# Identity products in free PSUM tiles, W^T copies behind both transposes, and a new written-out order in an RWKV-7 + cosine-gated MLP kernel

## The chip, the cores and the metric

One Trainium2 chip, one core. The time is the device time of one execution in microseconds (us). TensorE (PE; its weight loads are shown as PEld) multiplies into PSUM, VectorE (DVE) and ScalarE (ACT) read PSUM and write SBUF, GpSimd (POOL) works on SBUF, and SyncE (SP) and ACT issue the transfers between HBM and SBUF. Each engine takes its instructions in the order in which the program gives them; between engines they wait on semaphores.

## The reference

An attention block of the RWKV-7 kind with 4 batches, 8 heads, 768 steps and head dimension 40 runs first. Its output, as 3072 tokens of 320 values, goes through a two-layer MLP with h * cos(h) between the layers.

```
for t in range(S):
    y[t] = r[t] @ state
    Sa = state @ a[t]
    state = state * w[t] - outer(Sa, b[t]) + outer(v[t], k[t])
x = y as (3072, 320)
h = x @ w_in            # 320 -> 2048
out = (h * cos(h)) @ w_out   # 2048 -> 320
```

The MLP's weights come as 64-bit floats; everything is computed in 32-bit floats.

## The kernel before, in words

**Units.** The 768 steps are cut into chunks of 64 and the batches into pairs, which gives 24 units u; a unit is 64 steps of two batches, 128 partitions. Units 2n and 2n+1 make up group n, 256 tokens of the MLP. Within a chunk the recurrence is written as matrix products and one triangular inverse for each head.

**Segments of a unit.** `pw` (`p1_w`) transposes the decay w of two units; `pa` (`p1_a`) transposes a and multiplies it by w; `rw` (`over_w`) takes 1/w on DVE; `pb` and `pn` (`p1_b`, `p1_n`) transpose b over w and form the products of a and b, which fill the triangular systems; `inv` and the items `i` solve these on DVE for four units at a time, in 31 steps (the first four units in blocks of half the size, with the products `below` in `F` and `S` between); `H` and `R` add the lower blocks (tiles `beside`). Then come `v` and `k` (transposes of v, r and k), `g` (`gram`), `ag`, `xa`, `s`, `z` (the state of the next chunk and the output `yt`), `t` and `q` (the state transposed, times r). `T` and `X` bring `yt` to the MLP's layout `xT` by way of HBM, `Y` does it for the first two units on TensorE. `K` is work on POOL ahead of `k`.

**The decay.** For the first four units w is the plain input, and its running product is made by a scan on DVE behind the transpose; `p1_w` keeps both units of the pair in one tile `wT` of PSUM. For each unit of the pair in turn it transposes (four products against `ident`), copies or scans to `wb` in SBUF, and makes `wc` on POOL. From unit 4 on the running product along time is made beforehand in another layout (`scan`, `wj`, `sd`, `ws`: two sweeps on DVE and POOL, stored to HBM and loaded again), and `p1_w` copies the transposed tile to `wb` on ACT (line 371).

**Weights.** The 64-bit weights are rounded to 32 bits in 20 blocks of 512 columns. `f` fetches a block's words; the items `c` take the steps of `rounded` in the order of the list `w_names`: `taken` (sign on ACT, line 264; mantissa and exponent on DVE, lines 265 and 266; the exponent's power on ACT, line 269), `mantissa` (DVE, line 272), `product` (DVE, line 278; POOL, line 281). In the program's order `taken` of block n+2 stands behind `mantissa` of block n+1.

**The MLP.** Pieces `M` run in a fixed sequence: `first_a` and `first_b` (tiles `ph`, 256 tokens by 512 of the 2048 columns), then `second` (tiles `po`) for the piece before. The items `r` are the cosine and the product on ACT and DVE between them (`turns`, `gT`); `o` stores the output. A piece asserts that its weights are ready.

**PSUM.** Three pools of two tiles each: `ps_a` with tiles of two banks (tag `at`), `ps_h` and `ps_o` with one bank. `at` and `one` take a tile; the first writer waits until the last reader of the buffer's tile before is done.

**What sets the order.** The string `PLAN` is an order written out item by item; the loop at the end runs through it and emits each item's instructions, so an engine's order is that of the items. `L` items load a unit's inputs (`Lk3`: k of unit 3), by SP, or by ACT where the name ends in `a`. A transfer waits in its queue until its buffer is free, and what stands behind it in the queue waits too.

**TensorE's clock.** The profile lists a granted clock; it is 1.00 in most of the run and 0.50 in stretches of the first part.

Of the kernel before, what the change touches and what calls it, by code (L numbers as in the profile page):

```python
# [20 lines left out]
def kernel(  # L21
# [64 lines left out]
    G = {"rest": [], "outs": []}  # L86
# [150 lines left out]
    def rounded(m, dst, src):  # L237
# [23 lines left out]
        def taken():  # L261
            hi, mant = t["words"][:, :, 1], dst.bitcast(I32)
            t["sign"] = sb2.tile([P, DM], F32, tag="ot", name="sign").bitcast(BF16)[:, :WID]
            nc.scalar.activation(t["sign"], hi, ACTF.Sign)
            nc.vector.tensor_scalar(mant, hi, 0xFFFFF, None, ALU.bitwise_and)
            nc.vector.tensor_scalar(
                hi, hi, 20, 0x7FF, ALU.logical_shift_right, ALU.bitwise_and
            )
            nc.scalar.activation(hi, hi, ACTF.Relu, bias=to_bits, scale=2.0**23)
# [13 lines left out]
        return fetch, taken, mantissa, product  # L283

    def weights():
# [5 lines left out]
        def put(dst, src):  # L291
            if wide:
                work.append(rounded(len(work), dst, src))
                return

            def fetch():
                for rows, cols, part in src:
                    nc.sync.dma_start(dst[rows, cols], part)

            none = lambda: None  # L300
            work.append((fetch, none, none, none))
# [36 lines left out]

    def at(name):
        return ps_a.tile([P, 2, 512], F32, tag="at", name=name)  # L340

    def one(pool, name):
        if pool is None:
            return at(name)[:, 0]
        return pool.tile([P, 512], F32, tag="h" if pool is ps_h else "o", name=name)
# [12 lines left out]
    def p1_w(u):  # L358
        ps = at("wT")
        for i in range(2):  # L360
            turned(ps[:, i], nat["w", u + i])
            if u < 4:
                nc.scalar.copy(G["w1"][:, i, :, 0:1], b4(ps[:, i])[:, :, 0:1])
                nc.vector.memset(ps[:, i, ::C], 0.0)
            wb = ring.tile([P, 4 * P + 1], F32, tag="wb", name="wb")
            if u < 4:
                nc.vector.tensor_tensor_scan(
                    wb[:, 1:], ps[:, i], flat(G["w1"][:, i]), 0.0, ALU.mult, ALU.add
                )
            else:  # L370
                nc.scalar.copy(wb[:, 1:], ps[:, i])  # L371
# [476 lines left out]
    def first_a(g, j):  # L848
        assert not G["rest"]
        G["ph"] = [ps_h.tile([P, 512], F32, tag="h", name="ph").rearrange("p (f t) -> p f t", f=2)  # L850
                   for _ in range(2)]
# [53 lines left out]
    def second(g, j, i):  # L905

        if j == 0:
            G["po", i] = ps_o.tile([P, 512], F32, tag="o", name="po")
# [178 lines left out]
    with tc.manual_schedule():  # L1087

        w_work = weights()
        w_names = ["t0", "t1", "m0"]  # L1090
        follower = {4: 7, 5: 8, 6: 9, 11: 14, 12: 15, 13: 16, 14: 17, 15: 18, 17: 19}
        follower.update({m: m + 3 for m in range(7, 11)})
        for n in range(len(w_work)):
            w_names.append(f"p{n}")
            if n + 1 < len(w_work):
                w_names.append(f"m{n + 1}")
            if n + 2 < len(w_work):
                w_names.append(f"t{n + 2}")
        w_count = [0]

        def w_item():
# [6 lines left out]
            w_work[m]["tmp".index(name[0]) + 1]()  # L1108
# [27 lines left out]
        def inv_begin(q):  # L1136
# [8 lines left out]
            f1 pw0 Lk0 pa0 f3 pw2 pb0 pa2 pn0 lo0 pb2 inv0 pn2 i lo2 i i f0 i c Lv0 i i Lr0a K0 i f2 scan1 i  # L1145
            Lk1 i i c k0 v0 c i i i Lv1a i i g0 i wj1 i c K1 F0 ag0 c i F1 Lr1 c S1 S0 xa0 k1 H0 c f4 sd1 f5
            v1 c c R0 g1 F3 c s0 ag1 Lk2 c ws1 c c f6 Lv2 xa1 z0 K2 Lw4a s1 c S3 Lr2 Lb5a c c Y0 z1 c F2 c c
            k2 Y1 wf2 t2 c c c Lw5 v2 c S2 c Lb4 M c M La4 c r r La5 g2 r c r scan2 H1 c c r r c c Lv3 M pw4
            c rw5 ag2 q2 c rw4 M Lw7a c c xa2 R1 r M Lk3 c c r s2 c Lr3 c K3 r M pb4 r Lw6a z2 c r pa4 c wj2
            k3 c pn4 Lv4 r Lb6a c M Lb7 c rw7 v3 lo4 M Lk4 rw6 sd2 c g3 c T2 pw6 M La6a K4 r r t3 La7 c ag3  # L1150
            r q3 c c M pb6 xa3 c c c t4 c r r s3 Lr4 c c pa6 ws2 r z3 pn6 c c M c inv1 M c lo6 c r k4 X2 i r
            r i i T3 M v4 Lk5 r X3 i Lv5 i r i M r i i g4 M Lr5 i i M i r i Lr6 r wf3 ag4 i Lw9 q4 i r i r r
            M Lw8a i i M r t5 i M i Lb9a xa4 v5 M Lv6 i i r i i Lb8 r i i K5 M r i i r r i r i i i i k5 La8
            La9 q5 M Lk6 i pw8 M i g5 v6 M Lv7 H2 scan3 H3 r pa8 La11 rw8 R2 ag5 Lr7 r s4 M r Lb10 r rw9 z4
            Lw10 xa5 r wj3 M Lw11 r pb8 s5 K6 Lb11 M t6 pw10 rw10 sd3 pn8 La10 T4 pa10 lo8 ws3 M Lb12 rw11 r
            Lk7 r R3 z5 r inv2 pb10 X4 r La13 pn10 k6 M r r i La12 T5 X5 i g6 i M lo10 i i o K7 i i i ag6 q6
            Lw13 i i o Lb13a i i M v7 xa6 M r i r r i i s6 Lw12 r Lr8 t7 M i i M r i r k7 Lr9 z6 g7 Lk8 rw12
            M M i r r Lv8 wf4 i i ag7 q7 r i r M i xa7 i v8 K8 r o r M i k8 i i pw12 g8 T6 Lv9 rw13 t8 M M i
            i r Lv10 i i s7 i i Lk9 r pb12 i M ag8 r q8 r M r xa8 Lr10 H4 r pa12 z7 R4 M K9 Lw14 t9 v9 T7 X6
            Lk10 H5 s8 X7 M pn12 Lb15 scan4 Lw15 Lb14 r r z8 M Lv11 rw14 lo12 r M r r r k9 pw14 La14 g9 v10  # L1160
            M ag9 T8 wj4 q9 M o r La15 K10 Lk11 R5 Lb16 sd4 rw15 xa9 r M inv3 pa14 X8 k10 r M r r Lb17 g10
            s9 r M pb14 o Lr11 z9 pn14 M t10 r r r o i Lr12 i i M r M ag10 r i r Lv12 lo14 i T9 q10 M xa10 i
            M K11 i ws4 s10 v11 r M X9 i r M r La16 i r k11 Lw17 La17 r i r i i i i Lw16 z10 Lv13 g11 M M
            Lk12 r K12 pw16 i T10 Lr13 t11 r M i Lk13 i r M r ag11 i q11 r r i M i pa16 xa11 M r r rw16 r
            v12 i r i r v13 rw17 M M r Lr14 s11 i k12 La19 i i M M r z11 g12 r M wf5 r M i r r i r Lb18 pb16
            t12 i i i i i i M M X10 ag12 K13 q12 r i scan5 r Lk14 r M r Lw19 r r M H6 Lw18 xa12 inv4 M M T11
            R6 H7 r r r r r M s12 pn16 r M o k13 X11 lo16 M Lv14 t13 Lb19 La18 o v14 g13 z12 M r r ag13 K14
            T12 q13 r Lr15 r wj5 rw19 r M pw18 xa13 M k14 sd5 R7 pa18 r rw18 M t14 g14 s13 M r pb18 r Lv15 r
            z13 pn18 r M i r i ws5 Lk15 i i i K15 M i lo18 ag14 q14 r X12 i M v15 Lb20 i i xa14 i M i La21 r
            k15 s14 r i r M o Lv16 M r i i i T13 X13 r r i t15 Lk16 Lw21 i La20 g15 z14 Lr16 M i M r r ag15  # L1170
            q15 r i r i Lb21 Lr17 M M r o K16 r i v16 rw21 i Lw20 M k16 xa15 rw20 M r g16 i r r i s15 r Lk17
            Lb23 M i M T14 i r t16 r pw20 z15 i Lw22 pa20 M M r i ag16 q16 Lv17 r i M i r i i r r r Lr18 M
            Lv18 i t17 M i M xa16 r K17 v18 M pb20 r r H8 M Lk18 r r H9 R8 r T15 M M r s16 r r pn20 M lo20
            X14 M Lw23 Lr20 k17 X15 Lb22 o o inv5 v17 r r r z16 pw22 M T16 M r g17 R9 r r M K18 r ag17 r r
            Lk19 rw23 rw22 q17 M k18 M Lv19 La22 La23 M xa17 r X16 r r pa22 r r M M r o g18 s17 M pb22 z17
            pn22 M r r Lr19 i i lo22 r t18 r i i i K19 M M ag18 r r q18 i i M M xa18 r Lk20 i M i T17 r Lv20
            M r r r i X17 v19 v20 i r M t19 o s18 M r k19 i r z18 g19 r r M T18 r M r ag19 q19 M M i r xa19
            r i i r r M r Lv21 M r i i o K20 k20 i i M i i M g20 r Lr21 i s19 M i i r M r o r X18 r z19 r i
            t20 M Lv22 ag20 i i q20 M i r t21 Lk21 r r M M r Lr22 r T19 K21 i X19 i r i M xa20 M v22 r r v21
            M r i M i k21 i H10 r r Lk22 r M q21 Lr23 g21 M H11 r R10 r r M M ag21 r r s20 r M z20 xa21 M  # L1180
            s21 r T20 K22 r r X20 t22 r M M r k22 Lk23 z21 R11 r M Lv23 g22 M ag22 q22 r K23 r r o M o r T21
            r M X21 t23 r M xa22 M v23 r r r r k23 M r M s22 g23 r M ag23 q23 M xa23 r r r z22 s23 M r M r r
            M M r T22 z23 r r o o M X22 r M r r M M T23 r r r r M M r X23 r M M r r r r r r M M M M r r M r
            r r r M M o M r r M r r r o M r M M M r M r r r r r M o M o
# [16 lines left out]
        for n, (name, kind) in enumerate(zip(names, kinds)):  # L1201
            if kind == "M":
# [13 lines left out]
            else:  # L1216
# [6 lines left out]
                done.add(name)  # L1223
        assert not w_names and not inv_names and not G["rest"] and not G["outs"]
# [29 lines left out]
```

## Time and profile before

| what | value |
|---|---|
| median of 3 runs | 802.54 us (802.45 to 803.6) |
| the profiled execution | 800.9 us |
| its span, first to last instruction | 799.2 us |
| mean granted TensorE clock | 0.943 |
| PE busy | 730.2 us (91%), 11908 matmuls |
| DVE busy | 498.4 us (62%) |
| ACT busy | 416.4 us (52%) |
| POOL busy | 187.0 us (23%) |
| first piece of the MLP (`ph`) starts | 84.9 us |
| chain that ended last, by engine | PE 78%, DVE 11%, ACT 6%, issue 2%, DMA 2%, POOL 1% |

The page gives busy time by engine, the span in 40 slices (busy tenths and the granted clock), the chain of work that ended last, and groups of instructions. Lines of a timeline or chain start with the start in us and the length in us; "x32" is the number of instructions taken together. Most products are recorded at line 75 (`mm`) and transposes at line 350, so tiles' names tell the groups apart. A line of a wait reads: who waited, at which line, for whom, us in total, how many times, and the longest. In tables by stretches the numbers in brackets count instructions.

### The profile page before, as it was taken

To read this page: it belongs to the slowest core of one execution; us is meant where nothing else is said; L and a number is where in the kernel's file an instruction comes from. 1 tells how busy PE (TensorE), PEld (TensorE's weight loads), DVE (VectorE), ACT (ScalarE), POOL (GpSimd) and SP (SyncE) were. 2 spreads that over 40 slices of the span, in tenths; PEclk is the share of its full clock that TensorE was granted. 3 is DMA by queue.
4 is the path that set the end of the run, shared out by engine and by line. 5 is a ranking of instruction groups with operands and counts; after the bars stand their busy time and mean duration, and the time that the engine had idled before them with its cause. 6 is when DMAs were issued, how large, how long until landed. Compare 5 with 4: busy or idle time off the path is not lost.

```text
span 799.2 us, 27403 instructions
## 1 busy us (share of the span) xinstructions
PE 730.2 (91%) x11908; PEld 577.9 (72%) x11908; DVE 498.4 (62%) x965; ACT 416.4 (52%) x762; POOL 187.0 (23%) x320
## 2 busy tenths in 40 slices
PE   4568688899988999999999999999999999999995
PEld 4457566677776777877777777787878777777773
DVE  6686877698777864576864579733554863433221
ACT  1434656665474456563557464456464456454442
POOL 5244454320530233202232112221011012301000
PEclk8557898899899999999999999999999999999998
DMA  9444745553345204441322342321211210201000
GB/s 145 119 90 115 176 117 116 142 112 42 66 101 108 51 22 89 83 104 26 69 42 62 86 82 43 58 52 29 47 45 26 54 34 5 58 16 36 19 17 17
DMA packets 180912, 54.33 MB, mean 68 GB/s; under 512 B 156344, under 2 KB 176440, under 8 KB 180792
## 3 DMA queue, kind: packets, MB, share of 16 engines
q1 hardware_dynamic: 167000, 50.45, 28.8%
q10 hardware_dynamic: 13792, 2.13, 1.8%
q8 instruction: 94, 1.54, 0.8%
q14 instruction: 26, 0.21, 0.1%
HBM read 41.68 MB, written 10.81 MB: 66 GB/s over the span
## 4 chain that ended last, share of the span: by engine, by line
PE 78%; DVE 11%; ACT 6%; issue 2%; DMA 2%; POOL 1%; SPq 0%; ACTq 0%; DVEq 0%; POOLq 0%
PE ph L75 25%; PE po L75 24%; PE dps L75 4%; PE x0ps L75 4%; PE beside L75 3%; PE vT L350 2%; PE gram L75 2%; PE sps L75 2%; PE nps L75 2%; PE aps L350 1%; PE wT L350 1%; PE bT L350 1%; PE sT L690 1%; PE kT L350 1%; DVE inv L519 1%
## 5 line engine op out<-in xcount | busy, mean ns | idle before, releaser
L75 PE MATMUL po<-w_out_sb,gT 128*128 128x320 f32 x768 | 223.0, 441 | 0.0
L75 PE MATMUL ph<-xT,w_in_sb 128*128 128x256 f32 x768 | 185.4, 390 | 6.6 <-DVE gT L896 6.6
L75 PEld LDWEIGHTS po<-w_out_sb,gT 128*128 128x128 f32 x768 | 142.3, 191 | 57.4 <-issue 3.7
L75 PEld LDWEIGHTS ph<-xT,w_in_sb 128*128 128x128 f32 x768 | 142.8, 193 | 34.7 <-issue 14.1
L885 ACT ACTIVATE turns<-ph,rnd 128x512 f32<-128x512 f32 x96 | 62.6, 686 | 132.6 <-PE ph L75 130.2
L889 DVE SCALAR_TENSOR_TENSOR turns<-turns,ph 128x512 f32<-128x512 f32 x96 | 63.9, 681 | 84.5 <-ACT turns L885 84.4
L896 DVE TENSOR_TENSOR gT<-ph,turns 128x512 f32<-128x512 f32 x96 | 65.0, 686 | 45.9 <-ACT turns L893 45.8
L787 POOL TENSOR_TENSOR qz<-qz,wc 128x160 f32<-128x160 f32 x44 | 21.1, 482 | 227.9 <-DVE qz L786 226.2
L893 ACT ACTIVATE turns<-turns,half_pi 128x512 f32<-128x512 f32 x96 | 69.4, 723 | 3.1
L892 ACT ACTIVATE turns<-turns 128x512 f32<-128x512 f32 x96 | 60.4, 629 | 17.6 <-DVE turns L889 17.0
L519 DVE TENSOR_TENSOR inv<-inv,inv_tmp 128x31 f32<-128x31 f32 (+15 forms) x155 | 58.3, 376 | 5.3
L515 DVE TENSOR_TENSOR inv_tmp<-u,inv 128x31 f32<-128x31 f32 (+15 forms) x155 | 54.6, 352 | 3.1
L75 PE MATMUL ph<-xT,w_in_tail 64*64 64x256 f32 (+1 forms) x704 | 52.1, 384 | 0.0
L384 DVE RECIPROCAL rw<-nat_w 128x320 f32<-128x320 f32 x20 | 42.6, 2139 | 0.0
L802 POOL TENSOR_TENSOR yt<-yt,wb 128x512 f32<-128x512 f32 x24 | 31.7, 1321 | 42.0 <-DVE yt L797 42.0
L385 POOL TENSOR_TENSOR bn<-nat_b,rw 128x320 f32<-128x320 f32 x22 | 19.4, 882 | 92.1 <-DVE rw L384 54.1
L738 DVE COPY x<-x0ps 128x416 f32<-128x416 f32 x24 | 14.1, 587 | 39.2 <-ACT x L737 39.0
L760 DVE TENSOR_TENSOR sm<-sps,su 128x256 f32<-128x256 f32 x48 | 18.1, 419 | 30.9 <-ACT sm L755 28.8
L75 PEld LDWEIGHTS ph<-xT,w_in_tail 64*64 64x64 f32 (+1 forms) x704 | 26.8, 137 | 14.6 <-issue 9.3
L706 ACT COPY qz<-qps 40x512 f32<-40x512 f32 x44 | 25.5, 580 | 21.5 <-PE qps L75 21.1
L350 PE MATMUL wT<-ident,nat_w 128*128 128x128 f32 x88 | 15.0, 296 | 17.4 <-ACT wb L371 11.2
L598 POOL COPY rt<-rt 32x512 f32<-32x512 f32 x24 | 15.4, 641 | 58.0 <-DVE rt L523 54.1
(151 smaller groups left out, 1132.2 us busy)
## 6 DMA issues: line engine op xcount, KB each, us to landing
nat_k<-in_k_dram SPq DMA_DIRECT2D x48, 80.0 KB
out_dram<-ot SPq DMA_DIRECT2D x24, 160.0 KB
vp<-in_v_dram SPq DMA_DIRECT2D x92, 40.0 KB
rp<-in_r_dram SPq DMA_DIRECT2D x92, 40.0 KB
xd<-yt SPq DMA_DIRECT2D x44, 80.0 KB
nat_a<-in_a_dram SPq DMA_DIRECT2D x41, 80.0 KB
ws<-in_w_dram SPq DMA_DIRECT2D x5, 640.0 KB
wd<-ws SPq DMA_DIRECT2D x5, 640.0 KB
```

Source lines behind the costliest of these rows:

```text
L75: nc.tensor.matmul(o, lhsT=lhsT, rhs=rhs, start=start, stop=stop, skip_group_check=True)
L350: nc.tensor.transpose(ps[:, i * P : (i + 1) * P], x[:, 2 * i : 2 * i + 2].rearrange("p e d -> p (e d)"), ident)
L384: nc.vector.reciprocal(rw, wn)
L515: nc.vector.tensor_tensor(tmp, u[:, j : j + 1, :j].to_broadcast([P, Q - j, j]), x[:, j:, j : j + 1].to_broadcast([P, Q - j, j]), ALU.mult,)
L519: nc.vector.tensor_tensor(x[:, j:, :j], x[:, j:, :j], tmp, ALU.subtract)
L706: nc.scalar.copy(pick(z[rows], 0, (NZ - C, 2), (NZ, 2 * NB), (1, C)), ps[rows, :, : 2 * NB * C].rearrange("p f (i t) -> p f i t", t=C),)
L802: nc.gpsimd.tensor_tensor(yt.rearrange("p j b t -> p (j b) t"), yt.rearrange("p j b t -> p (j b) t"), wx, ALU.mult)
L885: nc.scalar.activation(n, u, ACTF.Identity, bias=rnd, scale=1.0)
L889: nc.vector.scalar_tensor_tensor(ns[e], ns[e], -ROUND, us[e], ALU.add, ALU.subtract)
L892: nc.scalar.activation(n, n, ACTF.Abs)
L893: nc.scalar.activation(n, n, ACTF.Sin, bias=half_pi, scale=-2.0 * math.pi)
L896: nc.vector.tensor_tensor(gT[:, 2 * e : 2 * e + 2].rearrange("p f t -> p (f t)"), us[e], ns[e], ALU.mult)
```

## The change

Four things change.

1. A new item `^` in the plan adds one to a counter. The next tile that `at` or `one` takes from PSUM is first written by as many products of the identity with four copies of itself (128x128 against 512 columns). The real products of the tile follow and write over it. The plan has 91 such items: 62 stand ahead of `k2`, 87 ahead of `inv1`, and the last ahead of `t9`. The tiles `ph` and `po` are now taken through `one`, too.
2. `p1_w` makes both units' transposes first and then the scans or copies of both.
3. `taken` is split: its second half, the exponent on DVE and the power on ACT, is an item of its own, `power` (named `e`). `w_names` now has `taken` of block n+2 ahead of `mantissa` of block n+1, and `power` of block n+2 behind it. There are 20 more items `c` and no more instructions for them.
4. The plan is another order of the same items. Most segments keep their sequence on TensorE, with neighbours exchanged; `Lv0` stands at the very front, `scan1` ahead of the first inverse's steps, the first fetches `f` behind `pn2`. Some loads change their queue, most of them from ACT to SP; ACT issues 18 transfers instead of 30.

```diff
-    G = {"rest": [], "outs": []}
+    G = {"rest": [], "outs": [], "turns": 0}
...
             nc.vector.tensor_scalar(mant, hi, 0xFFFFF, None, ALU.bitwise_and)
+
+        def power():
+            hi = t["words"][:, :, 1]
             nc.vector.tensor_scalar(
                 hi, hi, 20, 0x7FF, ALU.logical_shift_right, ALU.bitwise_and
             )
...
-        return fetch, taken, mantissa, product
+        return fetch, taken, power, mantissa, product
...
+    def busy(ps):
+        for _ in range(G["turns"]):
+            mm(ps, ident, pick(ident, 0, (0, 512 // P), (1, P)), True)
+        G["turns"] = 0
+
     def at(name):
-        return ps_a.tile([P, 2, 512], F32, tag="at", name=name)
+        ps = ps_a.tile([P, 2, 512], F32, tag="at", name=name)
+        busy(ps[:, 0])
+        return ps
 
     def one(pool, name):
         if pool is None:
             return at(name)[:, 0]
-        return pool.tile([P, 512], F32, tag="h" if pool is ps_h else "o", name=name)
+        ps = pool.tile([P, 512], F32, tag="h" if pool is ps_h else "o", name=name)
+        busy(ps)
+        return ps
...
         ps = at("wT")
         for i in range(2):
             turned(ps[:, i], nat["w", u + i])
+        for i in range(2):
             if u < 4:
...
-        G["ph"] = [ps_h.tile([P, 512], F32, tag="h", name="ph").rearrange("p (f t) -> p f t", f=2)
-                   for _ in range(2)]
+        G["ph"] = [one(ps_h, "ph").rearrange("p (f t) -> p f t", f=2) for _ in range(2)]
...
-            G["po", i] = ps_o.tile([P, 512], F32, tag="o", name="po")
+            G["po", i] = one(ps_o, "po")
...
-        w_names = ["t0", "t1", "m0"]
+        w_names = ["t0", "t1", "e0", "e1", "m0"]
...
             w_names.append(f"p{n}")
+            if n + 2 < len(w_work):
+                w_names.append(f"t{n + 2}")
             if n + 1 < len(w_work):
                 w_names.append(f"m{n + 1}")
             if n + 2 < len(w_work):
-                w_names.append(f"t{n + 2}")
+                w_names.append(f"e{n + 2}")
...
-            f1 pw0 Lk0 pa0 f3 pw2 pb0 pa2 pn0 lo0 pb2 inv0 pn2 i lo2 i i f0 i c Lv0 i i Lr0a K0 i f2 scan1 i
-            Lk1 i i c k0 v0 c i i i Lv1a i i g0 i wj1 i c K1 F0 ag0 c i F1 Lr1 c S1 S0 xa0 k1 H0 c f4 sd1 f5
-            v1 c c R0 g1 F3 c s0 ag1 Lk2 c ws1 c c f6 Lv2 xa1 z0 K2 Lw4a s1 c S3 Lr2 Lb5a c c Y0 z1 c F2 c c
...
+            Lv0 ^ ^ ^ ^ ^ pw0 pa0 ^ ^ ^ ^ ^ pw2 pb0 pa2 Lk0a inv0 scan1 ^ ^ ^ pn0 ^ ^ ^ ^ pb2 lo0 ^ ^ ^ ^ ^
+            pn2 i i i i Lr0 K0 Lk1a f0 f1 f2 i i lo2 i ^ ^ v0 i i i i i ^ k0 i i i c wj1 i ^ g0 f4 Lv1 c i ^
+            ^ ^ ^ ag0 c ^ ^ ^ F1 c F0 i xa0 K1 Lr1a S0 ^ ^ S1 f3 c f6 c k1 ^ ^ ^ F3 c ^ H0 c ^ ^ ^ ^ ^ v1 c
+            sd1 c c c Lv2 c ^ F2 c ^ ^ R0 ^ g1 La5a ^ s0 c c ^ ag1 xa1 c z0 c f5 ^ ^ s1 ws1 Lr2 ^ ^ ^ t2 c c
...
+            if kind == "^":
+                G["turns"] += 1
+                continue
```

More of the change, by code (lines that the diff above doesn't have):

```diff
@@ L300, in put @@
             none = lambda: None
-            work.append((fetch, none, none, none))
+            work.append((fetch, none, none, none, none))
         flat_out = w_out_sb.rearrange("p f n -> p (f n)")
@@ L1107, in w_item @@
                 needs({10: "H0", 11: "S3", 16: "H1"}[m])
-            w_work[m]["tmp".index(name[0]) + 1]()
+            w_work[m]["temp".index(name[0]) + 1]()
             if name[0] == "p":
@@ L1144 @@
         PLAN = """
-            f1 pw0 Lk0 pa0 f3 pw2 pb0 pa2 pn0 lo0 pb2 inv0 pn2 i lo2 i i f0 i c Lv0 i i Lr0a K0 i f2 scan1 i
-            Lk1 i i c k0 v0 c i i i Lv1a i i g0 i wj1 i c K1 F0 ag0 c i F1 Lr1 c S1 S0 xa0 k1 H0 c f4 sd1 f5
-            v1 c c R0 g1 F3 c s0 ag1 Lk2 c ws1 c c f6 Lv2 xa1 z0 K2 Lw4a s1 c S3 Lr2 Lb5a c c Y0 z1 c F2 c c
-            k2 Y1 wf2 t2 c c c Lw5 v2 c S2 c Lb4 M c M La4 c r r La5 g2 r c r scan2 H1 c c r r c c Lv3 M pw4
-            c rw5 ag2 q2 c rw4 M Lw7a c c xa2 R1 r M Lk3 c c r s2 c Lr3 c K3 r M pb4 r Lw6a z2 c r pa4 c wj2
@@ L1150 @@
[L1150 to L1184, printed above, removed]
+            Lv0 ^ ^ ^ ^ ^ pw0 pa0 ^ ^ ^ ^ ^ pw2 pb0 pa2 Lk0a inv0 scan1 ^ ^ ^ pn0 ^ ^ ^ ^ pb2 lo0 ^ ^ ^ ^ ^
@@ new lines @@
+            pn2 i i i i Lr0 K0 Lk1a f0 f1 f2 i i lo2 i ^ ^ v0 i i i i i ^ k0 i i i c wj1 i ^ g0 f4 Lv1 c i ^
+            ^ ^ ^ ag0 c ^ ^ ^ F1 c F0 i xa0 K1 Lr1a S0 ^ ^ S1 f3 c f6 c k1 ^ ^ ^ F3 c ^ H0 c ^ ^ ^ ^ ^ v1 c
+            sd1 c c c Lv2 c ^ F2 c ^ ^ R0 ^ g1 La5a ^ s0 c c ^ ag1 xa1 c z0 c f5 ^ ^ s1 ws1 Lr2 ^ ^ ^ t2 c c
+            Lw4a c c z1 c c ^ Y0 Lk2 c c Lb4 ^ S3 Y1 ^ ^ S2 Lw5 Lb5 c c K2 c c ^ ^ ^ v2 c c k2 ^ M c c rw5
+            Lv3 M r r Lk3a c r ^ ^ ^ g2 c r La4 c r ^ H1 c c c rw4 r ^ pw4 c ^ ^ M ^ ^ ag2 c M c c c wf2 q2
@@ new lines @@
+            r K3 ^ ^ ^ ^ M c c c xa2 t3 r Lr3 c c r pa4 r scan2 ^ pb4 c M Lw6 R1 r La7 Lb6 ^ ^ v3 c r c c c
+            s2 pn4 M c c c lo4 Lw7 rw6 k3 wj2 La6 c c c M c Lb7 g3 c z2 Lv4 r pw6 c r ^ ag3 r q3 c c rw7 T2
+            c M c c xa3 r c pa6 M c Lr4 r ^ s3 c ^ pb6 c c Lk4 r ^ z3 sd2 X2 pn6 c ^ M c K4 Lb8 T3 c c ^ ^ ^
+            M c lo6 r inv1 M c r i X3 ws2 r M k4 i i r r i i i i r v4 i i ^ M i i g4 Lr5 Lv5 M i r i Lw9 r r
+            i ^ t4 ag4 r M r i i Lw8 r i i i M q4 i M Lk5 i i M wf3 xa4 pw8 La9 La8 i i r Lr6 i r v5 M i i
@@ new lines @@
+            Lv6 r r r i M r i i K5 M Lb9 i i ^ k5 i i t5 Lv7 M r g5 H2 Lr7 M v6 r inv2 R2 scan3 rw9 pa8 r s4
+            ag5 q5 M rw8 r Lw11 r Lw10 Lk6 xa5 r H3 z4 La10 pb8 K6 La11 Lb11 M rw11 s5 Lb10 pn8 lo8 wj3 M T4
+            X4 rw10 z5 r pb10 r T5 M t6 pw10 r sd3 pa10 r R3 pn10 r i r o M lo10 La13 k6 X5 i i M v7 i i g6
+            M ws3 Lk7 ag6 Lb12 r K7 i r i o r i Lv8 Lb13 q6 Lk8 i i Lw13 M xa6 i r i i k7 M t7 Lr8 r i g7 s6
+            i r M Lw12 i z6 K8 rw13 ag7 M r Lv9 q7 i r M r Lk9 Lr9 i xa7 i pw12 i M i r r La12 t8 i v8 r s7
@@ new lines @@
+            i M wf4 k8 v9 i T6 rw12 i o i pa12 M i r z7 g8 M r M ag8 r r r i Lb15 i i K9 q8 i Lb14 r La15
+            Lw14 Lr10 i i i M pb12 xa8 o Lv10 M r H4 r r T7 H5 X6 M R4 ^ t9 r scan4 r s8 pn12 X7 rw14 lo12
+            Lw15 Lr11 M r z8 Lk10 La14 k9 M v10 R5 wj4 g9 K10 M inv3 r r ag9 r q9 r rw15 M xa9 r pw14 pa14
+            k10 Lk11 sd4 r M T8 ws4 Lv11 t10 Lw16 X8 g10 s9 M pb14 z9 pn14 i lo14 M r M r M i r i r i T9 K11
+            r r Lb17 v11 Lk12 i M Lv12 o ag10 i q10 i i i M i i xa10 i Lr12 r Lb16 k11 r r i rw16 r r M i M
@@ new lines @@
+            r g11 s10 M i M i z10 v12 Lw17 r r r i i La17 o X9 r r i La16 M i M r pw16 i t11 K12 Lv13 M Lr13
+            ag11 q11 i T10 i M i k12 M r r r i M rw17 r i r r i pa16 xa11 Lv14 i M i M g12 s11 M X10 t12 i
+            v13 r r La18 i z11 r r pb16 wf5 Lk13 M r T11 r o i i ag12 K13 q12 i Lw19 M M r xa12 H6 Lr14 M r
+            r H7 R6 r X11 M t13 R7 Lk14 r Lw18 r s12 M M scan5 r r pn16 z12 r o r lo16 r K14 M Lb19 M v14 r
+            rw19 La19 M k13 inv4 pw18 Lb18 Lr15 g13 Lv15 T12 k14 M Lk15 ag13 wj5 r sd5 r q13 rw18 M Lv16
@@ new lines @@
+            xa13 r r r g14 X12 M pa18 ws5 r s13 M pb18 z13 o pn18 M T13 Lr16 i i i t14 M r r i r r Lb21 lo18
+            M r i o i K15 i k15 r Lw20 i M ag14 q14 M i v15 r La21 Lv17 i xa14 Lr17 M i i Lb20 r r M r Lk16
+            r t15 i r g15 i M M i r r r ag15 i q15 r X13 r r M M M rw20 s14 i i M r xa15 i z14 K16 Lw21 Lb22
+            r r s15 M r i r r M i i T14 La20 t16 o i z15 rw21 Lk17 M M r v16 i v17 X14 r M r M r k16 i pw20
+            r Lw23 r i g16 i i Lr18 i pb20 o K17 M i i M r i ag16 r r r q16 r M Lw22 r i M i xa16 pa20 M M r
@@ new lines @@
+            r T15 r r H8 H9 M r M Lk18 t17 X15 pn20 k17 r M lo20 La23 M g17 r r q17 La22 inv5 r M r r R8 R9
+            M ag17 r s16 M M r o r Lr19 Lb23 z16 Lv18 r r xa17 r M M K18 r s17 rw22 rw23 v18 M k18 pw22 g18
+            pa22 M r T16 r pb22 r z17 pn22 o i i r r X16 M r M t18 lo22 M M Lk19 Lr20 ag18 T17 i r X17 r q18
+            r i M i i Lv19 M r r r xa18 M K19 Lv20 t19 i i i i Lk20 i s18 M r r r v19 i v20 r M Lr21 i M k19
+            r Lr22 r i i i z18 g19 M M r i r i ag19 q19 r r T18 M M r K20 xa19 r k20 M M r s19 i M r i r r r
@@ new lines @@
+            M o r z19 t20 i X18 Lv22 i M g20 M Lk21 r r i i r T19 X19 i M M r i ag20 r q20 Lv21 r o M K21 i
+            i xa20 i i i M i Lk22 r r t21 r r k21 M i M i v22 r v21 r M H10 g21 M Lv23 r Lr23 r o r R10 H11
+            r M M r ag21 r q21 M s20 xa21 M r r R11 r r z20 s21 M M K22 t22 r T20 X20 r z21 k22 M T21 g22 M
+            Lk23 r o K23 r X21 M M ag22 r r r r q22 M t23 xa22 M r r v23 r r r M M r k23 M g23 s22 M r ag23
+            r r q23 r r M M xa23 z22 r s23 M M T22 r o r r z23 X22 r r M r M M T23 M r X23 r r r M r M r M M
@@ L1185 @@
+            r r o r r M r M r M M r r r r M M r r o M M r r r M r o r r M M M r r r M r r r M M o M o
         """
@@ L1223 @@
                 done.add(name)
+        assert not G["turns"]
         assert not w_names and not inv_names and not G["rest"] and not G["outs"]
```

## The prediction

> **What bounds the kernel now.** I read the page's slices, then busy time by stretches, then the chain, then the waits.
>
> ```profile
> PE   4568688899988999999999999999999999999995
> PEclk8557898899899999999999999999999999999998
> ```
>
> In slices of 20 us TensorE is over nine tenths busy from about 160 us on; before that it has gaps and runs partly at half clock. The table by stretches (length, busy us of PE, PEld, DVE, ACT, POOL, granted clock, DMA share, GB/s):
>
> ```profile
> 16.00:48.00 32.00, 16.55 (x368) 14.39 (x368) 23.20 (x52) 11.38 (x28) 6.65 (x15) 0.55 0.59 141
> 48.00:70.00 22.00, 20.41 (x660) 18.17 (x664) 14.89 (x28) 9.28 (x19) 7.59 (x9) 0.50 0.37 101
> ...
> 160.00:260.00 100.00, 93.03 (x1493) 72.61 (x1496) 80.34 (x167) 56.43 (x107) 23.45 (x41) 0.95 0.43 86
> 260.00:800.00 540.00, 524.14 (x8036) 410.82 (x8026) 298.10 (x576) 282.38 (x507) 95.61 (x162) 0.99 0.22 47
> ```
>
> After 260 us TensorE's own work sets the end: 524 of 540 us at clock 0.99. So what counts is how early that state is reached, and each gap of TensorE behind it. Half clock nearly doubles a product; the same 32 products sps, before and after the clock came back at about 70.2 us:
>
> ```profile
> 64.85 2.03 PE L75 MATMUL sps<-x,rt 64*64 64x104 f32 x32 [0.55 <-ACT w_in_sb L572]
> 71.58 0.94 PE L75 MATMUL sps<-x,rt 64*64 64x104 f32 x32 [0.59 <-DVE x L738]
> ```
>
> The chain in time (start, us, what) shows these products on the path, and DVE in turn with them:
>
> ```profile
> 15.26 1.24 DVE wb L367
> 16.49 0.09 issue
> 16.58 1.09 PE wT L350 x4
> 17.67 1.71 PE bT L350 x8
> ...
> 52.24 1.91 PE below L75 x128
> 54.15 1.04 PE kT L350 x4
> 55.19 1.09 PE beside L75 x34
> ```
>
> And the waits, in us in total, times, longest; the first over the whole run, the others before 160 us:
>
> ```profile
> PE wT L350 <- ACT wb L371: 11.2, 10, 2.5
> ...
> DVE w_out_sb L266 <- ACT sign L264: 7.8, 5, 4.3
> DVE words L266 <- ACT sign L264: 7.1, 5, 3.6
> ```
>
> **The change part by part.** The profiled execution took 800.9 us (span 799.2); the median is 802.54, so 1.6 is added at the end.
>
> *Half clock before 160 us.* Stretches at clock 0.50 hold some 49 us of busy TensorE up to 160 us, and the first transposes, though shown at 1.00, run at the half-clock length (wT x4: 1.10 us against 0.66 later), 6.5 us more. On the chain are 27.1 us of them up to 85 us (1.1 + 1.1 + 6.2 from 16.58, 1.1, 2.0, then 3.7 and 11.9 from 48 to 64) and 12.4 us between 98 and 156. Row pairs give the saving: sps 2.03 to 0.94, x0ps 1.59 to 0.87, below 1.05 to 0.73; about 45% on the mix, or 17.8 us if all of it shows. DVE bounds this: from 48 to 60 us it is busy 10.1 of 12 us, so it takes over soon. I take 10, with ends 4 and 17.8.
>
> *Does the added work hold the clock?* In rows of 1 us the clock falls about 3.4 us after TensorE goes idle (idle from 91.7, low at 94.3) and returns only after dense stretches: after transposes from 16.6 to 22.7, after ph from 98.0 to 101.1, after dps from 152.0 to 155.7. From 48 to 67 us TensorE is over nine tenths busy, mostly with tiles of 32x32 and single transposes between, and it stays at 0.50. So small tiles count little, and 512-column products of a full 128x128 array should count fully. The Trainium skill (TensorE: Matmul & The Clock Gate, Part 1) has the clock open after one busy window of about 3.4 us; by that rule the stretch from 48 would have been at full clock from about 55 and the added products would be worth some 4 us less there. The trace disagrees: 20.41 of 22 us busy at 0.50, and the measurement decides.
>
> *The 91 products.* 128 columns take 0.11 us at full clock (kT, four in 0.44) and 0.2125 at half (wn, four in 0.85), so 512 columns are 0.44 and 0.85 us: 40 us in all at full clock, 77 at half. 87 stand before inv1 (some 160 us in the kernel before), where TensorE is idle 160 - 113 = 47 us and would be idle more with faster products. Hidden, they cost nothing; exposed, 0.44 each. They stand in order ahead of the real products of their tile, so where those are ready early, they hold them up. One case is visible: the first five can start when ident is ready (1.7 us) and last to 5.9, while nat_w lands at 4.3; transposes of w and the reciprocals behind them start later, 0.7 us net. The four and five ahead of pb2 and pn2 may push those by about 1 us. I take one in eight as exposed, 11 x 0.44 = 5 us, with ends 0 (all in gaps) and 15 (a third).
>
> *Copies after both transposes.* The second transpose of a pair waited for the first one's copy. In the first four units DVE's scan of unit 3 thus came at 18.10 instead of right behind that of unit 2 at 16.5, and the reciprocal behind it at 20.27; with both transposes done, the scans follow each other and the reciprocal starts near 17.8: 2.4 us of chain. I take 2, ends 0 and 3. Of the 11.2 us wait, 3.1 lie before 160 (I take 2) and 8.1 after, where TensorE is the bound: I take 7, ends 4 and 8.1. The price: the first copy now starts one group of transposes later, 0.44 us, and POOL's wc waits for it; POOL is busy 23% and nothing near is due, so 0, at most 1.
>
> *`taken` split in two.* DVE's shift waited for the sign on ACT, 14.9 us up to 160; behind it stood the inverse steps and turns. Now other items stand between. Same instructions (967 rows on DVE in both). Much of this idle time is off the chain; I take 3, ends 0 and 10.
>
> *New order, and loads on other queues.* ACT issues 18 transfers instead of 30: 12 x 0.63 = 7.6 us less of its time; SP has twelve more, but no row shows SP as the bound. One thing is queued worse: on SP the rows we<-ws, which wait for scan1, now stand ahead of rp and of the first words. Since scan1 comes ahead of the inverse (DVE waits 5.0 us for nt there at 25.5), they go at about 27 instead of 38; rp lands 1.9 us after its last issue, so by 32, when v0 wants it. Cost 0, ends -5 and +5, since no row shows the new order.
>
> *Half clock after 160 us.* About 10 us of products on the chain at 203.5 to 210.3 and 251 to 254.5, worth 4.5; no added products stand there, but fewer gaps lead up to it. I take 1.5, ends 0 and 4.5.
>
> Sum: -10 + 5 - 2 - 2 - 7 - 3 - 1.5 = -20.5. 800.9 - 20.5 = 780.4; with the 1.6 of the median, 782.
>
> **Rivals.**
> *The other engines take it.* TensorE is faster at first, but DVE and ACT chains (words, inverse, reciprocals) hold the first piece of ph where it is, 84.9 us, and only the waits for W^T go: -7 - 2 = -9, 793.5. For it: DVE is 74% busy up to 160. Against: it has 41 us idle there, and the chain's TensorE pieces from 48 to 64 have no other engine beside them at 60 to 64.
> *All of it shows.* All products in gaps, the whole half clock won: -17.8 - 2 - 2 - 8.1 - 6 - 3 = -39, 763.5. For it: a plan can place work in gaps exactly; against: DVE's share above.
> *Slower: the clock doesn't open and the products stand on the path.* If they don't count as activity (they multiply mostly zeros), 62 of them before k2 last 62 x 0.85 = 53 us. Real TensorE work up to 85 us is 43.5 us at half and 11.3 at full clock (some 20 at half): 53 + 64 + 1.7 puts the first ph at 118, 33 later; less 9, 826. It decides where exposed products eat the 25.5 us that the sum has without them: 30 of them at half clock (0.85), or 58 at full (0.44). Against: transposes against the same ident opened it at 22.7.
> *Nothing to measure.* Gain and exposed products cancel: 802.5.
>
> **How the numbers follow.** The sum's case 0.55, the other engines 0.22, all of it 0.10, slower 0.10, no change 0.03. A difference under 0.2% (1.6 us) can't be told from none in this kernel. Faster 0.55 + 0.22 + 0.10 = 0.87; same 0.03; slower 0.10. The likeliest is 782. The range 766 to 800 takes in the second rival's 793.5 with the first's spread, and leaves out the slower case and most of the best one. The ends of all terms together would give 751 to 816.
>
> **What would show it.** Right: granted clock 0.9 or more from 16 to 70 us (0.55 and 0.50 now) and mean over 0.97; 91 products of 128x512 at about 0.44 us spacing; the first ph at 73 to 79 us; no wait of wT for wb; sps under 1 us everywhere; TensorE's idle time after 160 us down by some 7. Wrong: clock still 0.5 in 16 to 70; products of 0.85 us; the first ph at or behind 85 us with DVE idle before it; or TensorE idle as long after 160 us for another reader of PSUM.

## The result and the profile after

The changed kernel takes 813.92 us (813.17 to 815.64) against 802.5 for the kernel before on the same chip: 1.0155 times as long, 95% interval 1.0115 to 1.0196. It is 1.6% slower. The prediction had 782 us, range 766 to 800, and gave "slower" one chance in ten.

The page of the changed kernel, with the lines that answer to those shown of before:

```profile
span 813.8 us, 27765 instructions
...
PE 786.4 (97%) x12090; PEld 587.0 (72%) x12090; DVE 504.9 (62%) x965; ACT 416.3 (51%) x762; POOL 183.9 (23%) x320
...
PE   8979999999999999999999999999999999999995
...
PEclk9979999999999999999999999999999999999998
...
PE 86%; ACT 5%; DVE 3%; DMA 2%; issue 2%; SPq 1%; POOL 1%; ACTq 0%; POOLq 0%
```

The clock did come back: 0.988 on the mean, against 0.943. TensorE is busy 786.4 us instead of 730.2, and its share of the chain that ended last went from 78% to 86%, while DVE's fell from 11% to 3%. TensorE's idle time fell from 69 to 27 us. So the gaps were filled and the clock held, and the kernel is longer.

The stretches of the changed kernel (length, busy us of PE, PEld, DVE, ACT, POOL, granted clock, DMA share, GB/s), and behind them the two of before that the prediction does not show:

```profile
16.00:48.00 32.00, 25.67 (x347) 15.07 (x345) 19.63 (x37) 8.44 (x25) 7.95 (x18) 0.98 0.52 128
48.00:70.00 22.00, 20.75 (x381) 10.98 (x382) 12.18 (x27) 4.41 (x9) 0.26 (x2) 0.80 0.28 74
70.00:85.00 15.00, 15.00 (x323) 8.31 (x324) 7.54 (x11) 6.63 (x12) 6.14 (x7) 1.00 0.20 58
85.00:121.00 36.00, 36.00 (x571) 22.37 (x562) 25.18 (x45) 14.64 (x27) 15.55 (x18) 1.00 0.47 102
```

```profile
70.00:85.00 15.00, 11.33 (x368) 9.50 (x360) 12.59 (x26) 6.92 (x14) 10.46 (x11) 0.99 0.37 89
85.00:121.00 36.00, 25.84 (x484) 20.34 (x485) 29.34 (x51) 23.62 (x39) 18.32 (x22) 0.91 0.63 149
```

From 70 to 121 us TensorE is now busy without a gap (before, 37.2 of these 51 us), and DVE and ACT get less done in the same time: ACT waits 21.1 us for TensorE there (6.7 before), DVE 7.3 (0.3 before). The timeline shows with what TensorE is busy (start, length, number of records):

```profile
1.71 6.43 PE L75 MATMUL wT<-ident 128*128 128x512 f32 x10 [1.71 <-POOL ident masks.py:199]
7.98 1.04 PE L364 MATMUL wT<-ident,nat_w 128*128 128x128 f32 x8
...
73.44 4.56 PE L75 MATMUL vT<-ident 128*128 128x512 f32 x10
77.84 0.60 PE L364 MATMUL vT<-ident,vp 128*128 128x128 f32 x4
...
80.32 1.98 PE L75 MATMUL beside<-ident 128*128 128x512 f32 x4
82.24 1.20 PE L75 MATMUL beside<-rt,half 32*32 32x32 f32 x64
```

Look at the counts. Five products of the identity stand ahead of `vT`, and the row has ten records: a product of 32-bit floats is recorded twice, a transpose once (`vT<-ident,vp` x4 for four transposes). The page's count says the same: 91 products raise the matmul records from 11908 to 12090, by 182. The transposes behind the five products start 4.40 us after them (73.44 to 77.84), so a product takes 0.88 us at full clock; the prediction had 0.44. By the groups of the profile all 182 records are busy 94.4 us, and the first real product of ph starts at 111.7 us instead of 84.9.

The waits of TensorE that the change aimed at are gone; after 160 us the longest are

```profile
PE wT L364 <- PE dps L75: 1.0, 1, 1.0
PE vT L364 <- DVE x L753: 0.6, 1, 0.6
```

where 8.1 us of waits for `wb` had been.

### The profile page after: what moved, and what is told of

It reads as the page before. It is cut to its first block, busy times and chain, and to the rows that moved or that the text cites. A ratio compares the mean times of both kernels' runs of the same rounds, so it can differ in the third digit from the quotient of the medians.

```text
span 813.8 us, 27765 instructions
## 1 busy us (share of the span) xinstructions
PE 786.4 (97%) x12090; PEld 587.0 (72%) x12090; DVE 504.9 (62%) x965; ACT 416.3 (51%) x762; POOL 183.9 (23%) x320
## 4 chain that ended last, share of the span: by engine, by line
PE 86%; ACT 5%; DVE 3%; DMA 2%; issue 2%; SPq 1%; POOL 1%; ACTq 0%; POOLq 0%
PE ph L75 26%; PE po L75 24%; PE x0ps L75 5%; PE dps L75 4%; PE beside L75 3%; PE gram L75 3%; PE sps L75 3%; PE vT L364 2%; PE below L75 2%; PE wT L75 2%; PE bT L364 1%; PE sT L705 1%; PE nps L75 1%; PE kT L364 1%; PE vT L75 1%
## 5 line engine op out<-in xcount | busy, mean ns | idle before, releaser
L75 PE MATMUL po<-w_out_sb,gT 128*128 128x320 f32 x768 | 220.4, 438 | 0.0
L75 PE MATMUL ph<-xT,w_in_sb 128*128 128x256 f32 x768 | 182.5, 385 | 0.8 <-DVE gT L910 0.5
L75 PEld LDWEIGHTS ph<-xT,w_in_sb 128*128 128x128 f32 x768 | 140.7, 190 | 30.9 <-issue 9.9
L802 POOL TENSOR_TENSOR qz<-qz,wc 128x160 f32<-128x160 f32 x44 | 21.1, 482 | 185.0 <-DVE qz L801 183.4
L688 DVE TENSOR_TENSOR ag<-gram,su 128x512 f32<-128x512 f32 x24 | 16.4, 685 | 36.2 <-PE gram L75 36.2
L653 POOL TENSOR_TENSOR kn<-nat_k,rw 128x320 f32<-128x320 f32 x24 | 22.2, 925 | 26.2 <-DMA nat_k<-in_k_dram 26.2
```

Source lines behind the costliest of these rows:

```text
L75: nc.tensor.matmul(o, lhsT=lhsT, rhs=rhs, start=start, stop=stop, skip_group_check=True)
```

## The experiments

Three theories. A: the products are too long, and most of them stand on the path. B: the new order itself loses. C, which came up beside A after the first runs: the faster clock in the opening is worth little, since other engines hold the first ph there. Times are medians; ratios are to the kernel before on the same chip, with 95% intervals.

### No products; half their columns

```diff
     def busy(ps):
-        for _ in range(G["turns"]):
-            mm(ps, ident, pick(ident, 0, (0, 512 // P), (1, P)), True)
         G["turns"] = 0
```

> The changed kernel without the 91 identity products; order, copies and split stay. Theory A (the products are too long: each is two records of about 0.43 us, 0.88 us at full clock, 94.4 us busy in all, and most of them stand on the path): the granted clock falls back to 0.5 in most of 16 to 70 us, gaps come back, and the time is 788 to 797 us, well below the changed kernel's 813.9 and by some 9 to 12 below the 802.5 of before (copies and split remain). Theory B (the new order itself loses, the products only fill what it leaves idle): 803 us or more, with first ph still behind 95 us.

Measured: 779.44 us, 0.9716 (0.9697 to 0.9735).

```diff
-            mm(ps, ident, pick(ident, 0, (0, 512 // P), (1, P)), True)
+            mm(ps[:, :256], ident, pick(ident, 0, (0, 256 // P), (1, P)), True)
```

> The same 91 products with 256 columns in place of 512: by the records 0.44 us each, the size that the prediction had assumed. Theory A: TensorE loses some 45 us of products, the clock stays at 0.9 or more between 16 and 85 us, and the time falls to 782 to 795 us. If it comes to 782, only the size was off. Theory B: within 3 us of the changed kernel's 813.9, since the idle time of the order would take the place of the columns. A third case: the shorter products no longer hold the clock; granted clock about 0.5 to 0.7 in 16 to 70 us and 795 to 805 us.

Measured: 781.62 us, 0.9743 (0.9723 to 0.9764).

B falls at once: without the products the same order is 23 us faster than the kernel before, better than any theory had it, with its clock low again (0.64 and 0.59 in the two stretches that follow). Without products:

```profile
16.00:48.00 32.00, 17.30 (x624) 14.50 (x626) 26.81 (x53) 12.32 (x31) 7.14 (x17) 0.64 0.68 150
48.00:70.00 22.00, 16.58 (x531) 14.86 (x523) 16.59 (x31) 10.01 (x20) 7.85 (x9) 0.59 0.37 90
```

With products of 256 columns:

```profile
16.00:48.00 32.00, 25.45 (x590) 20.48 (x594) 26.26 (x51) 12.30 (x31) 7.81 (x17) 0.88 0.62 137
48.00:70.00 22.00, 22.00 (x614) 17.51 (x606) 15.03 (x27) 8.68 (x18) 6.24 (x7) 0.86 0.46 111
```

The second table is what the prediction wanted to see: products of the length it had assumed, the clock near 0.9. No time is left of it: 781.6 against 779.4, with the first ph at 86.5 instead of 81.9 us. That the time is the predicted 782 is chance: products and clock come to +2.2 us where -5 was forecast, and everything else to -23 where -15.5 was.

### Each other part alone, in the old order

W^T's copies behind both transposes:

```diff
         for i in range(2):
             turned(ps[:, i], nat["w", u + i])
+        for i in range(2):
             if u < 4:
```

> The kernel before with one edit: both transposes of W^T ahead of the copies. By the prediction 2 + 2 + 7 = 11 us less, 791.5 us, range 790 to 797; the 11.2 us wait of wT for wb gone. Rival: another wait takes its place (the next user of the tile, or ACT later) and it gains under 3 us, 800 to 803.

Measured: 788.47 us, 0.9827 (0.9806 to 0.9848): 14 us, more than the 11 predicted. The wait of wT for wb on ACT is gone; the first inverse of four units starts at 28.2 instead of 30.5 us, the first ph at 82.2 instead of 84.9, and the first output tile is copied at 174.2 instead of 177.8. The two profiled executions differ by 11.0 us (spans 799.2 and 788.2): 3.6 of them are won by that tile and 7.4 behind it, where all of the 8.1 us of waits had been; a wait of sps for x grew there from 2.0 to 4.4 us.

The split of `taken`, with the same number of items in the plan:

```diff
-        w_names = ["t0", "t1", "m0"]
+        w_names = ["t0 e0", "t1 e1", "m0"]
...
-            if n + 1 < len(w_work):
-                w_names.append(f"m{n + 1}")
             if n + 2 < len(w_work):
-                w_names.append(f"t{n + 2}")
+                w_names.append(f"t{n + 2} m{n + 1}")
+                w_names.append(f"e{n + 2}")
+            elif n + 1 < len(w_work):
+                w_names.append(f"m{n + 1}")
```

> The kernel before with one edit: the rounding's first step split, its DVE shift and ACT power moved behind the next block's mantissa, in the same number of items. By the prediction 3 us less, 799.5 us (ends 0 and 10): DVE's wait for the sign, 14.9 us up to 160, nearly gone. Rival: that wait was off the path, 801 to 804 us; or, since the sign's step now stands ahead of a mantissa, DVE's order is worse and it takes 804 to 808.

Measured: 809.09 us, 1.0072 (1.0047 to 1.0097): 6.6 us slower, just beyond the 804 to 808 us of the rival. The profiled execution was the fastest of seven, at 803.88 us, so its rows show only a part of the loss. DVE's waits in it up to 160 us, where those for the sign had been 7.8 and 7.1:

```profile
DVE w_out_sb L269 <- ACT sign L264: 5.6, 3, 3.5
DVE u L510 <- ACT nt L464: 5.5, 1, 5.5
DVE x L741 <- ACT x L740: 5.2, 3, 4.0
```

The wait for the sign did shrink, to 5.6 and under 2, and the time grew; DVE waits longer for x (5.2 against 2.4) and TensorE for the first gT (8.7 against 6.4). A wait removed in an order made for another sequence of the items was not time won; which of the longer waits made the loss is not shown.

### The parts within the new order

The new order without products, and W^T's copies back between the transposes:

```diff
         for i in range(2):
             turned(ps[:, i], nat["w", u + i])
-        for i in range(2):
             if u < 4:
```

> The new order without products, with W^T's copies back between the two transposes: against 779.4 with the copies behind. The copies alone took 14 us off the old order (788.5). If the parts add up, 790 to 796 us; if the new order had by itself placed the waits elsewhere, 780 to 786 us.

Measured: 788.76 us, 0.9823 (0.979 to 0.9857), 9 us above 779.4 and between the two cases that were expected. The same without the split:

```diff
-
-        def power():
-            hi = t["words"][:, :, 1]
             nc.vector.tensor_scalar(
                 hi, hi, 20, 0x7FF, ALU.logical_shift_right, ALU.bitwise_and
             )
...
-        return fetch, taken, power, mantissa, product
+        return fetch, taken, lambda: None, mantissa, product
```

> The new order without products, with the power's two instructions back out of the program's place for them: its item `power` is empty and both stand at the end of `taken`. Against 779.4. If the split is worth the 3 us of the prediction in the order it was made for, 781 to 788 us; if it is as in the old order, where it lost 6.6 us, 770 to 777 us; if it doesn't matter, 779 to 780 us.

Measured: 786.92 us, 0.9799 (0.9769 to 0.9829), 7.5 us above. So in the order that was made for it the split is worth 7.5 us, and in the old one it costs 6.6. With the copies but without the split the new order (0.9799) can't be told from the copies alone in the old one (0.9827, the intervals meet): copies, split and order are one thing, worth 23 us together.

### How long the products may be, and how many

128 columns instead of 512, `mm(ps[:, :P], ident, ident, True)`:

> The changed kernel with products of 128 columns, two records of about 0.11 us each, some 20 us in all. Theory A (a faster clock in the opening is worth time, once the products are short enough): clock above 0.8 in 16 to 85 us and 768 to 776 us, below the 779.4 without products. Theory C (the opening is bounded by DVE and transfers, so the clock there is worth nothing and each product is at best free): 778 to 782 us, whatever the clock.

Measured: 778.72 us, 0.9697 (0.9665 to 0.9728), theory C's case: the clock is up (0.76 and 0.81), and the time is that of the run with no products.

384 columns:

```diff
-            mm(ps, ident, pick(ident, 0, (0, 512 // P), (1, P)), True)
+            mm(ps[:, :384], ident, pick(ident, 0, (0, 384 // P), (1, P)), True)
```

> All 91 products with 384 columns, about 0.66 us each at full clock and 63 to 70 us in all. Between 256 columns (781.6) and 512 (813.9). If the gaps hold about 45 us of products and what is over stands on the path nearly in full, 793 to 801 us, first ph at 95 to 100. If a single placement breaks only at 512 (the five ahead of nat_w, a transfer queue behind a late reader), 783 to 789 us.

Measured: 797.67 us, 0.9957 (0.9937 to 0.9978), as expected of products that no longer fit. Every fourth product at the full 512 columns:

```diff
-                G["turns"] += 1
+                G["turns"] += names[:n].count("^") % 4 == 0
```

> Every fourth of the 91 products at the full 512 columns: 23 products, 20 to 24 us in all, the same TensorE time as 91 of 128 columns (778.7). If only the total counts, 777 to 782 us; if a single long product costs by itself where it stands, 785 us or more. The clock in 16 to 70 us should be lower than with 91 of them, 0.6 to 0.8.

Measured: 775.58 us, 0.9675 (0.9649 to 0.9702), below either case, with a higher clock than expected. Every eighth (`% 8`), and every fourth with 256 columns:

> Every eighth product at 512 columns, 12 products, some 12 us. If the number of places matters, the clock in 16 to 70 us falls to 0.65 to 0.75 and the time is 777 to 779 us; if 12 still hold it, 773 to 776 us.

> Every fourth product at 256 columns, 23 products, some 11 us. If length holds the clock, it falls below the 0.85 and 0.90 of the full length in 16 to 48 and 48 to 70 us and the time is 777 to 780 us; if a place with any product is enough, the clock stays and the time is 772 to 775 us, since TensorE is given less to do.

Measured: 781.51 us, 0.9736 (0.971 to 0.9762), and 776.13 us, 0.9675 (0.9647 to 0.9703). The first lies above both of its cases, the second between its two.

| products | busy with them, us | clock 16-48, 48-70 us | first ph, us | time, us | ratio to before |
|---|---|---|---|---|---|
| none | 0 | 0.64, 0.59 | 81.9 | 779.4 | 0.9716 |
| 12 of 512 columns | 17.8 | 0.70, 0.58 | 84.1 | 781.5 | 0.9736 |
| 23 of 256 | 19.6 | 0.74, 0.76 | 80.3 | 776.1 | 0.9675 |
| 23 of 512 | 29.2 | 0.85, 0.90 | 81.0 | 775.6 | 0.9675 |
| 91 of 128 | 35.7 | 0.76, 0.81 | 83.8 | 778.7 | 0.9697 |
| 91 of 256 | 55.0 | 0.88, 0.86 | 86.5 | 781.6 | 0.9743 |
| 91 of 384 | 76.4 | 0.90, 0.83 | 101.1 | 797.7 | 0.9957 |
| 91 of 512 (the change) | 94.4 | 0.98, 0.80 | 111.7 | 813.9 | 1.0155 |

The second column is the sum over the groups of products in each profile, so it holds products at half clock, too; it is a little high, since the last record of a group is shown as running on beside the next instruction (73.44 + 4.56 is past 77.84). Up to 55 us the products change the time by no more than 4 us either way. Above, most of it is on the path: from 55.0 to 76.4 us, 21.4 more, the time grows by 16.1; from 76.4 to 94.4, 18.0 more, by 16.2. Theory A holds, and it is not one bad placement that breaks only at 512 columns. With 384 and 512 columns the loss is in the opening: of the 34.5 us that the change's products cost (36.2 between the two profiled executions), 29.8 are there at the first ph.

TensorE's time up to the first ph shows why. Here each record counts from its start to the next one's:

| products | TensorE's own work, us | products, us | idle, us | first ph, us |
|---|---|---|---|---|
| none | 51.8 | 0 | 30.1 | 81.9 |
| 23 of 512 columns | 40.1 | 19.5 | 21.4 | 81.0 |
| 91 of 256 | 38.1 | 36.2 | 12.2 | 86.5 |
| 91 of 512 (the change) | 36.6 | 63.7 | 11.5 | 111.7 |

At the faster clock TensorE's own work is 12 to 15 us shorter, and the idle time falls from 30 to some 12 us and no further. By these rows, and as an estimate, that is room for about 33 us of products ahead of the first ph. What goes beyond it, some 3 us with 256 columns and 30 with 512, is near what ph starts later by, 4.6 and 29.8.

Which part of the plan they stand in, tried with 256 columns: only those behind `k2`, then only those ahead of it.

```diff
-                G["turns"] += 1
+                G["turns"] += "k2" in done
```

> Only the 29 products behind `k2`, 256 columns each (about 13 us). With all 91 of this length the first ph came 4.6 us later than with none, but the end only 2.2 us later, so those behind `k2` should gain some 2 us of their own: 776 to 778 us, against 779.4 with none. If the products are never worth anything, 779 to 782 us.

> Only the 62 products ahead of `k2`, 256 columns each (about 30 us, the clock up in the opening). If the opening is bounded by DVE and transfers, they only cost: first ph at 86 to 87 us and 782 to 785 us. If the clock in the opening is worth its 10 us once the products behind `k2` are gone, below 777 us.

Measured: 780.12 us, 0.9728 (0.9698 to 0.9757), and 780.19 us, 0.9731 (0.9702 to 0.9761). Neither can be told from none (0.9716) or all (0.9743); the first is what was expected if the products are worth nothing, the second lies between its two cases. The early ones bring the first ph to 86.2 us, 4.3 later than without, and nearly all of that is made up by the end; by what is not shown.

### What holds the clock

```diff
-            mm(ps, ident, pick(ident, 0, (0, 512 // P), (1, P)), True)
+            mm(ps[:32, :256], ident[:, :32], pick(ident, 0, (0, 256 // P), (1, P)), True)
```

> The 91 products of 256 columns again, but of only 32 columns of the identity (a quarter of the array): the same length on TensorE, less of the array at work. If small tiles don't hold the clock, as the prediction read it, the clock is 0.5 to 0.65 in 16 to 70 us while the products take as long or longer. Theory A: the clock's worth goes and the products' length stays, 790 us or more against 781.6 with the full array. Theory C: 780 to 785 us. If the clock is as with the full array, the reading that small tiles count little is wrong.

Measured: 784.07 us, 0.9764 (0.9731 to 0.9797), with the clock at 0.95 and 0.84 in the two stretches. A quarter of the array's columns holds the clock as well as the whole. The prediction's "small tiles count little" is therefore not about the number of array columns in use. The stretch from 48 us that stayed at 0.50 also used a quarter of the rows (tiles of 32x32), and its products there were far shorter (16 and 32 columns); which of these properties counts was not tried.

### Does DVE hide the clock's worth?

`mantissa` left out, with every fourth product and with none:

```diff
-            nc.vector.scalar_tensor_tensor(
-                dst, t["words"][:, :, 0].bitcast(U32), 2.0**-32, dst.bitcast(I32),
-                ALU.mult, ALU.add,
-            )
+            pass
```

> Every fourth product at 512 columns, and the rounding's step `mantissa` left out: 20 instructions of 0.68 us on DVE, 13.6 us in all, some 6 of them ahead of the first ph. The low words of the weights aren't added, so the weights are cut to powers of two. If DVE holds the opening, the first ph comes 3 us or more before the 81.0 us that it has with the step, and the time is 768 to 772 us. If something else holds it (transfers, TensorE), within 1 us of 81.0 and 773 to 777 us.

> The same without any product. The difference to the run with every fourth is the clock's worth when DVE has less to do: more than 3.9 us (5 to 9) if DVE had hidden it, so 776 to 779 us here while the other falls; the same 3 to 4 us if it hadn't. If both fall alike, DVE is a bound but not what hid the clock.

Measured: 772.55 us, 0.9621 (0.9591 to 0.965) with products and 772.85, 0.9621 (0.9592 to 0.9649) without. Without products the time falls by 6.6 us, so DVE's work is part of the bound; with them by 3.0, where the intervals just meet. The first ph came at 82.4 us with products (81.0 with the step in), later than either case had it, and at 79.7 without (81.9), and the gap between the two vanished instead of growing. Products and clock together gain nothing here either. That DVE's rounding hid the clock's worth is not shown. Nor is it refuted: in the run with products and without `mantissa` the clock itself was lower (0.79 and 0.77 in the two stretches, 0.85 and 0.90 with the step in).

What stands ahead of the first ph can be read in the run with every fourth product, where it starts at 80.96 us. First the chain up to TensorE's `below` at 78.03 (start, us, what):

```profile
71.30 0.70 ACT sign L264
72.00 0.02 issue
72.03 0.43 DVE words L269
72.46 0.60 DVE w_out_sb L281
73.06 0.66 DVE yt L812 x2
73.72 0.46 DVE qz L801 x2
74.18 0.46 DVE w_in_sb L265
...
76.24 0.68 DVE words L269
76.92 0.86 DVE w_out_sb L281
...
78.03 0.79 PE below L75 x54
```

Then TensorE's own rows up to ph:

```profile
74.33 1.10 PE L75 MATMUL below<-ident 128*128 128x512 f32 x2 [0.60 <-DVE qz L801]
75.36 0.73 PE L75 MATMUL below<-rt,w_in_sb 32*32 32x16 f32 x64
76.01 1.75 PE L75 MATMUL xps<-yt,eye 128*128 128x128 f32 x14
78.03 0.73 PE L75 MATMUL below<-rt,w_in_sb 32*32 32x16 f32 x64 [0.27 <-DVE rt L599]
78.69 1.12 PE L75 MATMUL vT<-ident 128*128 128x512 f32 x2
79.65 0.60 PE L364 MATMUL vT<-ident,vp 128*128 128x128 f32 x4
...
80.96 3.62 PE L75 MATMUL ph<-xT,w_in_sb 128*128 128x256 f32 x16
```

Up to 78.03 the chain runs over DVE and ACT, on the weights and the state. But TensorE is only 0.27 us ahead of it there: from 74.33 to 80.96 it is busy 6.36 of 6.63 us, and two products of the identity (1.03 and 0.96 us from start to start) are part of that. Both engines hold the first ph at nearly the same time, so taking work from DVE alone could move it little. With `mantissa` out TensorE goes on almost without a gap from 75.83 to ph at 82.36. Theory C's times hold, then, but its reason only in part: besides the other engines, the products themselves take up what the clock frees.

## Why the prediction was wrong

**The step that failed is the price of the 91 products.** It took 0.44 us for 512 columns from the row of `kT`, four transposes in 0.44 us. Those are one record each; a product of 32-bit floats is two. The chain of before had the right row, too (start, us, what):

```profile
258.74 0.44 PE kT L350 x4
...
306.65 4.50 PE po L75 x16
```

The 16 records of `po`, 320 columns each, belong to eight products (two halves of four), 0.56 us each, and 512/320 of it is 0.90 us. Measured: 0.88 us, which is 80 us for 91 at full clock where the prediction had 40; with those that ran at half clock it came to 94.4. The Trainium skill (FP8 and Floating Point Precision, TensorE Precision Notes) gives a true 32-bit product four passes through the array. At the 2.4 GHz that the Trainium skill (TensorE: Matmul & The Clock Gate, Part 1) gives the open clock, that is an estimate of 0.85 us for 512 columns; the trace agrees, with 0.88.

The room that the prediction compared this with was right in kind: 47 us idle up to 160 us, more with faster products. Some 40 us of products would have fitted and 94 don't; the runs put the border between 55 and 76 us of the first table. "One in eight exposed" (5 us) thus became 34.5 us, net of what the clock gave. The slower rival named the point that decides (exposed products of 25.5 us, 58 at its price and 29 at the measured one) but tied its case to a clock that doesn't open. The clock opened, and the products stood on the path by their length alone.

**Half clock before 160 us**, 10 us gained (ends 4 and 17.8): not seen as a gain. The runs that raise the clock in the opening and keep the products short (91 of 128 or 256 columns, 23 of 256 or 512) lie between 3.9 us below and 2.2 above the run with none, and with `mantissa` out the difference is 0.3. TensorE's own work did shrink: up to the first ph from 51.8 us without products to 40.1 with every fourth. But the products that raised the clock took 19.5 us there, and only 8.7 of them went into idle time. The prediction counted the clock's gain and the products' cost as two terms; in these runs they take each other's place. How much the clock would be worth if it came free is open, since no run has it without products. The warning "DVE takes over soon" is borne out in part: in the run with every fourth product DVE's chain reaches ph at nearly the same time as TensorE's.

**The clock's behaviour** was right in the main: products of the identity hold it, 0.98 and 0.80 in the two stretches (0.9 had been asked of both). The reading about small tiles was wrong as far as the array's columns go. The clock's fall "about 3.4 us" after TensorE goes idle is misread: from 91.7 to 94.3 are 2.6 us. Two smaller misreadings change nothing: DVE is 75% busy up to 160 us, with 40 us idle (74 and 41), and has 965 rows (967).

**Copies after both transposes**, 11 us in three terms: mechanism right, 14.0 us alone. **The split**, 3 us (ends 0 and 10): 7.5 in the new order, outside the ends on the other side in the old one (-6.6). **The new order**, 0 (ends -5 and +5): alone it can't be told from 0, but without it the split loses. **Half clock after 160 us**, 1.5: from 160 to 260 us the clock is 1.00 in the changed kernel and in the run with no products, 0.95 before, so it came without the products. Together these are worth 23 us where the prediction's terms (2, 2, 7, 3 and 1.5) give 15.5. TensorE's idle time after 160 us fell from 22.0 to 14.7 us, the 7 that the prediction had named.

**The first five products** were to end at 5.9 us; they end at 8.1, and the transposes of w for both units behind them at 9.0; in the kernel before the first unit's ended at 5.6 and the second's at 8.4. The load queue came later than priced, too: we<-ws goes out at 32.0 us, not 27, with rp and the words behind it.

Products and clock together were forecast at -5 and came to +34.5, 39.5 us worse; everything else was 7.5 us better than its terms. That leaves the 32 us by which 813.9 lies above 782.

**A version that beats both kernels** is the change with no products (779.4 us), or with every fourth of them (775.6 and 776.1 for two lengths). Between these the intervals overlap, and every eighth lies at 781.5, above them all: that a few products help is not settled.

## What to carry to other kernels

Price an added instruction by a row of the same kind and look at the count of its records: in this profile a 32-bit product has two and a transpose one, a factor of two in time for the same columns. Filler on an in-order engine is free only while its total stays under the idle time that it can fall into and the time that it frees, some 33 us ahead of the first ph here; sweep its length before taking the clock it buys for a gain. And a clock that is bought with added work is worth what it frees less what the work takes: with 23 products TensorE's own work up to the first ph fell by 11.7 us, the products took 19.5, and ph came 0.9 us earlier.

## What the runs showed of the hardware that was not expected

A product that uses 32 of the array's 128 columns holds the granted clock like a full one (0.95 and 0.84 against 0.88 and 0.86, both at 256 columns). And 23 products of 0.88 us, spread over the first 160 us or so, lift the clock from 0.64 and 0.59 to 0.85 and 0.90, nearly what 91 do (0.98 and 0.80).
